# Attention and two feed-forward layers on one core: the second pair's operands in pieces, and two transpose banks lent as a third score buffer

## The chip, the cores and the metric

The kernel runs on one core of a Trainium2 chip. The metric is device microseconds (us) of one execution. Five engines work side by side, each through its own instruction queue in order: PE (TensorE, matmuls and transposes), DVE (VectorE), ACT (ScalarE), POOL (GpSimd) and SP (SyncE, which issues nearly all DMA transfers). PSUM, where PE writes, has eight banks of 128x512 float32; ACT and DVE read it.

## The reference

Attention over 4 batches of 8 heads (576 positions, head size 64), with rotary embedding of q and k, and then two feed-forward layers over the 2304 tokens.

```python
q_rot, k_rot = (rotate(q), rotate(k))            # x1*cos - x2*sin, x1*sin + x2*cos
scores = scale * np.matmul(q_rot, k_rot.transpose(0, 1, 3, 2))
attn = np.exp(scores - np.max(scores, axis=-1, keepdims=True))
attn = attn / (np.sum(attn, axis=-1, keepdims=True) + 1e-09)
x = np.matmul(attn, v)                           # then tokens x 512
...
h = x @ w_in;  g = s * np.maximum(h, 0)**2 + b;  x = g @ w_out        # 512 -> 2048 -> 512
g = x @ w_gate; silu = g / (1 + np.exp(-g)); x = (silu * (x @ w_val)) @ w_out2   # 512 -> 1536 -> 512
```

## The kernel before

Every float32 product is made from rounded halves: a value is split into a high part (fp32r) and the rest, and the products of the parts are added in PSUM. The 32 heads are worked as 16 pairs. For a pair p the steps are:

- **Preparation** (`prep`). q and k are loaded (tile x) and turned by the rotary tables (`rope`: four tensor operations, on DVE for the first pair, on POOL for the others) into the tile ry. PE transposes ry in three groups g = 0, 1, 2 of three blocks each (line 578, PSUM tile pst). For pair 0, ACT and DVE write the three operand tiles a (queries), t and kz (keys) straight from PSUM (lines 610 to 615). For all other pairs ACT writes the high part (qkhi, line 585) and DVE the rest (qklo, line 587), and SP then spreads them over the partitions with five DMA transfers a, a, t, t, kz (line 632). The operand tiles exist twice, for even and odd pairs.
- **Scores** (`pair`). A pair has nine chunks u = 0 to 8 of 128 queries. For each, PE multiplies a by t and kz (line 707: four matmuls 128x288, eight for u = 4) into a score buffer ps_s of two banks, DVE takes the row maximum (line 710, nm), ACT the exponential with its row sum (line 714, e). The buffer is free when ACT has read it.
- **Thirds** (`third`). For each three chunks PE transposes e back (lines 782 and 785: three groups of four 128x128 blocks and one of three 64x128) into a transpose bank ps_t; ACT writes the high part ph (line 790), DVE the rest (line 795: pl, or ph for the 64-row group); then the bank is free. PE multiplies by the values vh (lines 832 and 834, ps_av), ACT takes the result out (xr), SP stores it.

The eight banks are: three for transposes (`ps_t`, shared by the transposes of preparation and thirds, and later by feed-forward products), one for the values' product (`ps_v`), four for two score buffers (`ps_s`), which later become four accumulators of the feed-forward layers.

The order of instructions on every engine is not that of the code. A planner (`Schedule.run`) plays the program through with estimated durations, gives each engine the ready operation with the lowest priority number, hands out buffers by counting tokens, and emits the instructions in the order that comes out. A change in a buffer count or an operation's length therefore moves instructions all through the attention part. Short dummy matmuls (`warm`, line 463) fill PE at the start; eight each are tied behind chunk 1 and chunk 3 of the first pair. When the last pairs run out, first-layer products (hb, lines 938 to 940) fill PE; from there on PE has work without a break.

Of the kernel before, what the change touches and what calls it, by code (L numbers as in the profile page):

```python
# [187 lines left out]
def tile_attention_moe_moe(  # L188
# [54 lines left out]
        "xr": 2, "rbx": 1, "s": 2, "t": 3, "v": 1, "wx": 4, "gb": 2, "rb2": 3,  # L243
# [10 lines left out]
    ps_t = ctx.enter_context(tc.tile_pool(name="ps_t", bufs=3, space=PSUM))  # L254
# [5 lines left out]
    rp_p = early.enter_context(tc.tile_pool(name="rp", bufs=2, side="right"))  # L260
    att = ExitStack()
# [208 lines left out]
    first_rope, behind_rope, sts = [], [], {}  # L470

    qk_ops = list(sch.ops)

    def prep(p):
# [43 lines left out]
        for g in range(G):  # L518
# [8 lines left out]
            def r1(g=g, e=e, views=views, cs=cs):  # L527
                if g == 0:
                    take_ry()
                e.tensor_tensor(out=views(1)[1], in0=views(0)[0], in1=table(2, 1, cs.start, cs.stop), op=ALU.mult)  # L530
# [8 lines left out]
            if o is None and p:  # L539
                def y0():  # L540
                    take_ry()
                    if p == 1:
                        nc.gpsimd.tensor_copy(st["ryt"][:, 0, 0:1], first_rope[1]["ryt"][:, PC - 1, 2 * D - 1:2 * D])
                    nc.gpsimd.tensor_tensor(out=views2(0)[1], in0=views2(1)[0], in1=table(3, 1, 0, PC), op=ALU.mult)
# [35 lines left out]
            acq = (ps_tok, hi_tok if p else tok) if g == 0 else (ps_tok,)  # L580
# [26 lines left out]
            else:  # L607
# [15 lines left out]
                st.setdefault("a", []).append([o2, op("dve", t_dve(CG), sub(a[dn], a[up], up), prt + 3 * later, (o2,), (), (ps_tok,))])  # L623
                if p or g == 0:
                    ops += st["a"][-1]
        if p:
# [9 lines left out]
            ops = [  # L636
# [38 lines left out]
    def pair(p, st):  # L675
# [10 lines left out]
        for u in range(NU):  # L686
            pr = base + 10 * u
            s_tok = Token("s")
# [8 lines left out]
            def s_mm(u=u, terms=terms):  # L697
# [4 lines left out]
                ps = ps_s.tile([128, 1024], F32, tag="s", name="ps_s")  # L702
# [25 lines left out]

        sums[b]["exps"] += exps.values()
        if pp == H // 2 - 1:  # L730
# [7 lines left out]
            def r2():  # L738
                sums[b]["ps"] = ps_t.tile([128, 512], F32, tag="t", name="psr")
# [6 lines left out]
            tok, cr_tok = Token("t"), Token("cr")  # L746
# [14 lines left out]
        def third(y, pr):  # L761
# [11 lines left out]
            for i in range(4):  # L773
                t_tok = Token("t")
# [3 lines left out]
                def tr(i=i, part=part):  # L778
                    ps = st["pt", y, i] = ps_t.tile([128, 512], F32, tag="t", name="ps_t")
# [242 lines left out]

    def switch_0():
# [14 lines left out]
    def get_hb(tok, n):  # L1038
        p, tag = (ps_t, "t") if tok.pool == "t" else (ps_v, "v")
        return p.tile([128, 512], F32, tag=tag, name="hb")[:, 0:n]  # L1040
# [17 lines left out]
    def block_b():  # L1058
# [9 lines left out]
        fin = moe1(st, UB, range(F1), outs, x_toks, xp, prio, ("t", "v"), get_hb,  # L1068
# [166 lines left out]
    def block_s(i):  # L1235
# [19 lines left out]
        acc_tok = {(h, d): Token("t", "v") if (h, d) == (1, 0) else Token("acc") for h in range(2) for d in range(KD)}  # L1255
# [54 lines left out]
        def unit(u, pr):  # L1310
            t_g, t_5, t_m = (Token("rb2", "rc", "dec") for _ in range(3))
            banks, ps, prod = {x: Token("t", "v") for x in "xyz"}, {}, {}
# [174 lines left out]
    def block_2(i):  # L1487
# [27 lines left out]
        def bank(tok):  # L1515
            p, tag = (ps_t, "t") if tok.pool == "t" else (ps_v, "v")
            return p.tile([128, 512], F32, tag=tag, name="hb")[:, 0:QN]
# [49 lines left out]
        def unit(f, pr):  # L1567

            t_g, t_u, t_c, t_5 = (Token("rb2", "rc", "dec") for _ in range(4))
            banks, ps, prod = {x: Token("t", "v") for x in "xyz"}, {}, {}  # L1570
# [179 lines left out]
```

## Time and profile before

| | |
|---|---|
| median of 3 runs | 1081.68 us (1081.45 to 1081.71) |
| the profiled execution | 1081.71 us, its span 1079.9 us |
| PE busy | 1069.0 us, 99% of the span |
| DVE busy | 879.0 us, 81% |
| ACT busy | 732.0 us, 68% |
| POOL busy | 244.7 us, 23% |
| granted TensorE clock | 1.00 |

1.8 us lie around the span. The attention part is roughly the first 290 us; the rest belongs to the feed-forward layers. Busy time of PE counts each matmul to its modelled end, so that short gaps between matmuls of the attention part count as busy.

### The profile page before, as it was taken

To read this page: it belongs to the slowest core of one execution; us is meant where nothing else is said; L and a number is where in the kernel's file an instruction comes from. 1 tells how busy PE (TensorE), PEld (TensorE's weight loads), DVE (VectorE), ACT (ScalarE), POOL (GpSimd) and SP (SyncE) were. 2 spreads that over 40 slices of the span, in tenths; PEclk is the share of its full clock that TensorE was granted. 3 is DMA by queue.
4 is the path that set the end of the run, shared out by engine and by line. 5 is a ranking of instruction groups with operands and counts; after the bars stand their busy time and mean duration, and the time that the engine had idled before them with its cause. 6 is when DMAs were issued, how large, how long until landed. Compare 5 with 4: busy or idle time off the path is not lost.

```text
span 1079.9 us, 17714 instructions
## 1 busy us (share of the span) xinstructions
PE 1069.0 (99%) x6220; PEld 976.2 (90%) x6220; DVE 879.0 (81%) x1548; ACT 732.0 (68%) x1505; POOL 244.7 (23%) x239
## 2 busy tenths in 40 slices
PE   9999999999999999999999999999999999999998
PEld 8899998999888899999888888999989999899996
DVE  6899999999889999889999998876596675966751
ACT  6999999999978776556666556655565555655550
POOL 7997877887520000000000000000000000000000
PEclk9999999999999999999999999999999999999999
DMA  5766857656579655663566744311331222311102
GB/s 155 237 211 222 268 172 264 205 171 191 147 222 280 162 170 174 184 190 105 169 191 214 227 157 156 107 69 59 98 88 40 60 69 87 100 40 48 50 1 58
DMA packets 111593, 157.07 MB, mean 145 GB/s; under 512 B 34496, under 2 KB 67280, under 8 KB 111504
## 3 DMA queue, kind: packets, MB, share of 16 engines
q1 hardware_dynamic: 110688, 155.15, 46.2%
q8 instruction: 49, 0.80, 0.3%
q10 hardware_dynamic: 816, 0.79, 0.2%
q14 instruction: 40, 0.33, 0.1%
HBM read 99.98 MB, written 32.58 MB: 123 GB/s over the span
## 4 chain that ended last, share of the span: by engine, by line
PE 89%; ACT 4%; DVE 4%; issue 1%; DMA 1%; POOL 0%; SPq 0%; ACTq 0%; DVEq 0%
PE hb L938 14%; PE hb L940 14%; PE hb L939 14%; PE acc L939 6%; PE acc L940 6%; PE acc L938 5%; PE ps_s L707 5%; PE acc L1532 5%; PE acc L1533 5%; PE acc L1531 5%; PE ps_t L782 4%; PE ps_av L832 3%; PE ps_av L834 2%; ACT e L714 2%; ACT ph L790 1%; DVE pl L795 1%
## 5 line engine op out<-in xcount | busy, mean ns | idle before, releaser
L939 PE MATMUL hb<-w 128*128 128x384 f32 (+1 forms) x728 | 250.0, 343 | 0.0
L938 PE MATMUL hb<-w 128*128 128x384 f32 (+1 forms) x728 | 250.0, 343 | 0.0
L940 PE MATMUL hb<-w 128*128 128x384 f32 (+1 forms) x728 | 249.9, 343 | 0.0
L938 PEld LDWEIGHTS hb<-w 128*128 128x128 f32 x728 | 136.7, 188 | 8.4 <-ACT tmp L1592 0.2
L939 PEld LDWEIGHTS hb<-w 128*128 128x128 f32 x728 | 136.6, 188 | 7.5
L940 PEld LDWEIGHTS hb<-w 128*128 128x128 f32 x728 | 136.7, 188 | 4.4
L710 DVE TENSOR_REDUCE nm<-ps_s 128x1 f32<-128x576 f32 x144 | 108.0, 752 | 10.6 <-PE ps_s L707 9.3
L714 ACT ACTIVATE e<-ps_s,nm 128x576 f32<-128x576 f32 x144 | 107.4, 746 | 11.3 <-DVE nm L710 10.4
L790 ACT ACTIVATE ph<-ps_t 128x512 fp32r<-128x512 f32 (+1 forms) x183 | 101.2, 570 | 8.8 <-PE ps_t L782 7.3
L939 PE MATMUL acc<-gl,w 128*128 128x512 f32 (+1 forms) x288 | 106.0, 368 | 0.0
L940 PE MATMUL acc<-gh,w 128*128 128x512 f32 (+1 forms) x288 | 105.9, 368 | 0.0
L938 PE MATMUL acc<-gh,w 128*128 128x512 f32 (+1 forms) x288 | 105.9, 368 | 0.0
L707 PE MATMUL ps_s<-t,a 128*128 128x288 f32 x320 | 98.0, 323 | 2.0 <-ACT e L714 1.5
L832 PE MATMUL ps_av<-ph,vh 128*128 128x384 f32 (+1 forms) x320 | 96.5, 331 | 1.0 <-ACT xr L845 0.8
L795 DVE TENSOR_TENSOR pl<-ps_t,ph 128x512 fp32r<-128x512 f32 x135 | 90.0, 683 | 6.7 <-ACT ph L790 5.5
L1592 ACT ACTIVATE tmp<-hb 128x384 f32<-128x384 f32 x144 | 70.4, 489 | 34.5 <-PE hb L940 33.3
L707 PE MATMUL ps_s<-kz,a 128*128 128x288 f32 x320 | 88.9, 294 | 0.0
L782 PE MATMUL ps_t<-ident,e 128*128 128x128 f32 x576 | 85.5, 273 | 1.9 <-DVE pl L795 1.0
L782 PEld LDWEIGHTS ps_t<-ident,e 128*128 128x128 f32 x576 | 68.2, 141 | 8.8 <-DVE pl L795 1.9
L1230 DVE TENSOR_TENSOR w<-sums,w 128x512 fp32r<-128x512 f32 x104 | 68.4, 686 | 7.8 <-ACT w L1228 7.6
L834 PE MATMUL ps_av<-pl,vh 128*64 128x384 f32 (+1 forms) x256 | 72.3, 295 | 0.1
L1624 ACT ACTIVATE tmp<-tmp 128x384 f32<-128x384 f32 x72 | 37.7, 523 | 43.6 <-DVE tmp L1597 43.4
(145 smaller groups left out, 2478.1 us busy)
## 6 DMA issues: line engine op xcount, KB each, us to landing
raw<-gv SPq DMA_DIRECT2D x36, 512.0 KB, 3.7
raw<-in_moe_w_out_dram SPq DMA_DIRECT2D x28, 512.0 KB, 4.2
x_d<-xr SPq DMA_DIRECT2D x64, 144.0 KB, 2.5
raw<-in_moe_w_in_dram SPq DMA_DIRECT2D x16, 512.0 KB, 5.0
raw<-up SPq DMA_DIRECT2D x16, 512.0 KB, 4.3
raw<-in_moe_w_gate_dram SPq DMA_DIRECT2D x12, 512.0 KB, 4.8
raw<-in_moe_w_val_dram SPq DMA_DIRECT2D x12, 512.0 KB, 4.3
gv<-dec SPq DMA_DIRECT2D x24, 256.0 KB, 2.6
```

Of the source, the lines that this page charges most:

```text
L707: nc.tensor.matmul(ps[:, hf * 512:hf * 512 + HS], a[:, q0:q0 + 128], m[:, k0:k0 + HS], start=y == 0, stop=y == len(todo) - 1)
L710: nc.vector.tensor_reduce(out=st["nm"][:, u:u + 1], in_=st["s", u], axis=AX.XY, op=ALU.max, negate=True)
L714: nc.scalar.activation(out=st["e", u].rearrange("p (f n) -> p f n", f=2), in_=st["s", u], func=AF.Exp, bias=st["nm"][:, u:u + 1], accum_ou ...
L782: nc.tensor.transpose(ps[:, z * 128:z * 128 + 128], st["e", u][:, kc * 128:kc * 128 + 128], ident)
L790: nc.scalar.activation(out=st["ph", y][0:rows, 512 * i:512 * i + n], in_=st["pt", y, i][0:rows, 0:n], func=AF.Copy)
L795: nc.vector.tensor_tensor(out=dst, in0=st["pt", y, i][0:rows, 0:n], in1=st["ph", y][0:rows, c].bitcast(F32), op=ALU.subtract)
L832: nc.tensor.matmul(ps, vv, st["ph", y][:, c], start=kc == 0, stop=kc == 4, skip_group_check=True)
L834: nc.tensor.matmul(ps[0:64], vv[:, 0:64], st["pl", y][:, c], start=False, stop=False, skip_group_check=True)
L938: nc.tensor.matmul(o, lh, rh, start=first, stop=False, skip_group_check=more)
L939: nc.tensor.matmul(o, lh, rl, start=False, stop=False, skip_group_check=more)
L940: nc.tensor.matmul(o, ll, rh, start=False, stop=last, skip_group_check=more)
L1592: nc.scalar.activation(out=st[key, f], in_=ps[name], func=AF.Copy)
```

## The change

- **A third score buffer at first.** Of the three transpose banks one remains (`ps_t`). The two others are at the start one more score buffer, `ps_s0`, on the other side of PSUM. The transposed groups 1 and 2 of pair 0 go into its two halves; then chunk 2 of pair 0 uses it as its score buffer. When that chunk's exponential has read it, a switch (`switch_s0`) closes it and opens a pool t2 of two transpose banks, so that from there on there are three again; an operation takes one from t or t2, whichever is free (`BANKS`).
- **The second pair in pieces.** The rope of pair 1 runs on POOL as 3 x 4 operations, one set for each group, in place of four over all groups (a one-element copy that ordered it behind the first pair's rope remains), so that a group's transposes need its own four alone. Its spread transfers are 3 x 5, each for a group's 192 positions of both heads, and each needs its own group alone. Within a group the order is t, t, kz, a, a. The last group's two transfers of a are awaited by chunk 1 in place of chunk 0.
- **The order of pair 0's last subtractions on DVE** is set: t of group 2 ahead of a of group 1.
- Everything after takes the new names of the banks; the work of the feed-forward layers is the same.

```diff
-        "xr": 2, "rbx": 1, "s": 2, "t": 3, "v": 1, "wx": 4, "gb": 2, "rb2": 3,
+        "xr": 2, "rbx": 1, "s": 2, "s0": 1, "t": 1, "v": 1, "wx": 4, "gb": 2, "rb2": 3,
...
-    ps_t = ctx.enter_context(tc.tile_pool(name="ps_t", bufs=3, space=PSUM))
+    ps_t = ctx.enter_context(tc.tile_pool(name="ps_t", bufs=1, space=PSUM))
...
+    first_s = ExitStack()
+    ps_s0 = first_s.enter_context(tc.tile_pool(name="ps_s0", bufs=1, space=PSUM, side="right"))
...
+    def t_tile(tok, name):
+        return (ps_t if tok.pool == "t" else late[tok.pool]).tile([128, 512], F32, tag="t", name=name)
...
+            if p == 1:
+                def begin():
+                    take_ry()
+                    nc.gpsimd.tensor_copy(st["ryt"][:, 0, 0:1], first_rope[1]["ryt"][:, PC - 1, 2 * D - 1:2 * D])
+                if g == 0:
+                    o = op("pool", 0.1, begin, pr, (*lds[0], *rt_op, *first_rope[:1]), (ry_tok,))
+                for y, fn in enumerate((r0, r1, r2, r3)):
+                    o = op("pool", t_pool(fd if y > 1 else fd // 2), fn, pr + g, (o,), (), (x_tok,) if y == 3 else ())
+                st["rope"] = o
...
-            ps_tok = Token("t")
-            def tr(g=g):
-                st["ps", g] = ps = ps_t.tile([128, 512], F32, tag="t", name="pst")
+            if p == 0 and g:
+                ps_tok = s0_tok
+            else:
+                ps_tok = Token(*BANKS)
+            def tr(g=g, ps_tok=ps_tok):
+                if ps_tok is s0_tok:
+                    if g == 1:
+                        st["s0"] = ps_s0.tile([128, 1024], F32, tag="s", name="ps_s0")
+                    ps = st["s0"][:, 512 * (g - 1):512 * g]
+                else:
+                    ps = t_tile(ps_tok, "pst")
...
+                if g == 1:
+                    st["a1"] = st["a"][-1][1]
+                if g == G - 1:
+                    ops[-2].next.append(st["a1"])
+                    st["a1"].need += 1
...
-            ops = [
+            def piece(o, i, g):
+                return sch.dma(
+                    256 * 2 * S // G, lambda: nc.sync.dma_start(out=place(o, g).bitcast(F32), in_=place(i, g).bitcast(F32)), pr + 6 + g,
+                    (trs[g], *cleared), (tok,) if not ops else (), (hi_tok,), pace=1.1
+                )
+            for g in range(G if p == 1 else 0):
+                ops.append(piece(t[ev], lo_x[od], g))
+                ops.append(piece(t[od], hi_x[od], g))
+                ops.append(piece(kz[ev], hi_x[od], g))
+                ops.append(piece(a[ev], hi_x[ev], g))
+                ops.append(piece(a[od], lo_x[ev], g))
+            ops = ops or [
...
+        if p == 1:
+            st["a"], ops = ops[-2:], ops[:-2]
...
-            s_tok = Token("s")
+            s_tok = Token("s0" if p == 0 and u == 2 else "s")
...
-                ps = ps_s.tile([128, 1024], F32, tag="s", name="ps_s")
+                ps = (ps_s0 if p == 0 and u == 2 else ps_s).tile([128, 1024], F32, tag="s", name="ps_s")
...
+            if p == 1 and u == 1:
+                main = [*main, *st["a"]]
...
+        if p == 0:
+            op("sp", 0.0, switch_s0, -500, (exps[2],))
...
+    def switch_s0():
+        first_s.close()
+        pool("t2", 2, space=PSUM, side="right")
```

What the planner makes of it is shown at three places. The rows are instructions in queue order, with the line in the kernel's own file, the written tile, the tiles read and the shape.

The first place is DVE behind the first pair's operands: the maxima nm of pair 0 and the low parts qklo of pair 1. Before:

```order
L710 TENSOR_REDUCE nm<-ps_s 128x1 x5
L795 TENSOR_TENSOR pl<-ps_t,ph 128x512
L587 SCALAR_TENSOR_TENSOR qklo_184<-pst,ident,qkhi_182 128x2x192
L710 TENSOR_REDUCE nm<-ps_s 128x1
L587 SCALAR_TENSOR_TENSOR qklo_184<-pst,ident,qkhi_182 128x2x192 x2
L710 TENSOR_REDUCE nm<-ps_s 128x1
L795 TENSOR_TENSOR pl<-ps_t,ph 128x512 x2
L710 TENSOR_REDUCE nm<-ps_s 128x1
L795 TENSOR_TENSOR ph<-ps_t,ph 64x384
L710 TENSOR_REDUCE nm<-ps_s 128x1
```

Of the change:

```order
L752 TENSOR_REDUCE nm<-ps_s 128x1 x2
L611 SCALAR_TENSOR_TENSOR qklo_187<-pst,ident,qkhi_185 128x2x192
L752 TENSOR_REDUCE nm<-ps_s 128x1 x3
L611 SCALAR_TENSOR_TENSOR qklo_187<-pst,ident,qkhi_185 128x2x192
L752 TENSOR_REDUCE nm<-ps_s 128x1
L841 TENSOR_TENSOR pl<-ps_t,ph 128x512 x2
L752 TENSOR_REDUCE nm<-ps_s 128x1
L841 TENSOR_TENSOR pl<-ps_t,ph 128x512
L611 SCALAR_TENSOR_TENSOR qklo_187<-pst,ident,qkhi_185 128x2x192
L752 TENSOR_REDUCE nm<-ps_s 128x1
L841 TENSOR_TENSOR ph<-ps_t,ph 64x384
L752 TENSOR_REDUCE nm<-ps_s 128x1
```

Both pieces end with the maximum of pair 0's last chunk; in the change three pl, one ph and one pl follow, and then the maximum of pair 1's chunk 0. The first group of pair 1 has moved from behind chunk 4's maximum to between those of chunks 1 and 2, the second group ahead of the first third. On ACT the high part of the first group stands likewise between the exponentials of chunks 0 and 1, and on PE the group's transposes stand in the middle of the eight dummy matmuls behind chunk 1.

The second place is PE at the start of pair 2 (operands a_175, t_177, kz_179 before, a_178, t_180, kz_182 in the change). Before:

```order
L707 MATMUL ps_s<-t_177,a_175 128x288
L707 MATMUL ps_s<-kz_179,a_175 128x288
L707 MATMUL ps_s<-t_177,a_175 128x288
L707 MATMUL ps_s<-kz_179,a_175 128x288
L782 MATMUL ps_t<-ident,e 128x128 x4
L832 MATMUL ps_av<-ph,vh 128x384
L834 MATMUL ps_av<-pl,vh 64x384
L782 MATMUL ps_t<-ident,e 128x128 x4
```

Of the change:

```order
L828 MATMUL ps_t<-ident,e 128x128 x8
L749 MATMUL ps_s<-t_180,a_178 128x288
L749 MATMUL ps_s<-kz_182,a_178 128x288
L749 MATMUL ps_s<-t_180,a_178 128x288
L749 MATMUL ps_s<-kz_182,a_178 128x288
L749 MATMUL ps_s<-t_180,a_178 128x288
L749 MATMUL ps_s<-kz_182,a_178 128x288
L749 MATMUL ps_s<-t_180,a_178 128x288
L749 MATMUL ps_s<-kz_182,a_178 128x288
```

Before, chunk 0 of pair 2 stood ahead of five groups of pair 1's 128-row transposes and two 64-row groups, and these lay between the chunks of pair 2. Now all of pair 1's transposes but one 64-row group stand ahead of chunk 0, and chunks 0 and 1, then 2 and 3, follow each other. At the start of pair 3 both orders have issued the same work: 24 groups of 128-row transposes, 7 of 64 rows, 43 products with the values, 15 groups of preparation.

The third place is PE behind the last chunk of the last pair, where hb is the first layer's product. Before:

```order
L785 MATMUL ps_t<-ident,e 64x128 x3
L938 MATMUL hb<-x,w 128x512
L939 MATMUL hb<-x,w 128x512
L940 MATMUL hb<-x,w 128x512
L938 MATMUL hb<-x,w 128x512
L939 MATMUL hb<-x,w 128x512
L940 MATMUL hb<-x,w 128x512
L832 MATMUL ps_av<-ph,vh 128x192
L834 MATMUL ps_av<-pl,vh 64x192
L782 MATMUL ps_t<-ident,e 128x128 x4
```

Of the change:

```order
L831 MATMUL ps_t<-ident,e 64x128 x3
L828 MATMUL ps_t<-ident,e 128x128 x4
L878 MATMUL ps_av<-ph,vh 128x192
L880 MATMUL ps_av<-pl,vh 64x192
L878 MATMUL ps_av<-ph,vh 128x192
L880 MATMUL ps_av<-pl,vh 64x192
L828 MATMUL ps_t<-ident,e 128x128 x4
```

Twelve hb products that stood among the last third's transposes now stand behind them. In the feed-forward layers the order of PE's products changes in the first half and is the same from the middle to the end.

## Rows read from the trace of the kernel before

**Rows 1.** Stretches: length, busy time and instructions by engine, clock, DMA share, GB/s.

```profile
12.00:30.00 18.00, 16.39 (x130) 13.70 (x129) 14.07 (x23) 12.81 (x32) 17.84 (x13) 1.00 0.54 176
30.00:45.00 15.00, 14.46 (x117) 13.71 (x116) 13.72 (x23) 13.26 (x32) 14.18 (x12) 1.00 0.62 205
45.00:62.00 17.00, 16.69 (x133) 15.52 (x132) 15.38 (x25) 15.51 (x37) 17.00 (x11) 1.00 0.68 207
80.00:280.00 200.00, 197.43 (x1539) 183.99 (x1540) 187.45 (x295) 188.96 (x449) 158.16 (x163) 1.00 0.66 209
300.00:350.00 50.00, 50.00 (x223) 41.39 (x222) 44.65 (x74) 41.59 (x71) 5.92 (x7) 1.00 0.84 253
```

**Rows 2.** Waits, 13 to 64 us, DVE and ACT: total, times, longest.

```profile
DVE nm L710 <- PE ps_s L707: 3.2, 3, 1.6
ACT e L714 <- DVE nm L710: 5.5, 6, 2.1
```

**Rows 3.** Timeline, first pair: start, length, engine, line, operation, count, idle before.

```profile
13.53 1.42 DVE L710 TENSOR_REDUCE nm<-ps_s 128x1 f32<-128x576 f32 x2
14.32 0.74 ACT L714 ACTIVATE e<-ps_s,nm 128x576 f32<-128x576 f32 x1 [2.07 <-DVE nm L710]
15.20 0.40 PE L707 MATMUL ps_s<-t,a 128*128 128x288 f32 x1
16.03 1.49 DVE L710 TENSOR_REDUCE nm<-ps_s 128x1 f32<-128x576 f32 x2 [1.09 <-PE ps_s L707]
16.65 1.15 PE L463 MATMUL warm<-a 128*64 128x64 f32 x16
19.11 0.76 DVE L710 TENSOR_REDUCE nm<-ps_s 128x1 f32<-128x576 f32 x1 [1.59 <-PE ps_s L707]
20.04 0.58 ACT L585 ACTIVATE qkhi<-pst,ident 128x384 fp32r<-128x384 f32 x1
20.78 0.61 DVE L587 SCALAR_TENSOR_TENSOR qklo<-pst,ident,qkhi 128x384 fp32r<-128x384 f32 x1
```

**Rows 4.** Timeline of POOL: rope of pair 1 (first and last operation), clearing of kz.

```profile
10.31 1.41 POOL L544 TENSOR_TENSOR ry<-x,rt 128x576 f32<-128x576 f32 x1
15.88 2.69 POOL L552 TENSOR_TENSOR ry<-x,ry 128x1152 f32<-128x1152 f32 x1
34.42 1.14 POOL L629 MEMSET kz<- 128x1216 f32 x1
```

**Rows 5.** Pair 1's spread, first and last issue; a small load's KB and us to landing.

```profile
23.23 0.57 SPq L632 DMA_DIRECT2D a<-qkhi  x1
26.75 0.60 SPq L632 DMA_DIRECT2D kz<-qkhi  x1
vr<-in_v_dram SPq DMA_DIRECT2D x32, 80.0 KB, 2.5
```

**Rows 6.** Timeline: DVE at pair 0's end; PE at chunks 1.0, 2.0, 2.5.

```profile
28.44 1.29 DVE L795 TENSOR_TENSOR pl<-ps_t,ph 128x512 fp32r<-128x512 f32 x2 [0.68 <-ACT ph L790]
29.76 0.55 DVE L795 TENSOR_TENSOR ph<-ps_t,ph 64x384 fp32r<-64x384 f32 x1
...
31.04 0.38 PE L707 MATMUL ps_s<-t,a 128*128 128x288 f32 x1
...
45.06 0.38 PE L707 MATMUL ps_s<-t,a 128*128 128x288 f32 x1
...
55.32 0.29 PE L707 MATMUL ps_s<-t,a 128*128 128x288 f32 x1
```

**Rows 7.** Timeline, last pair: chunk 8, first hb, an ACT copy, the last transposes.

```profile
279.20 0.40 PE L707 MATMUL ps_s<-t,a 128*128 128x288 f32 x1
282.25 0.47 PE L938 MATMUL hb<-x,w 128*128 128x512 f32 x1 [0.26 <-DVE pl L795]
284.61 0.60 ACT L801 ACTIVATE raw<-ps_t 128x512 f32<-128x512 f32 x1 [1.31 <-PE ps_t L782]
288.33 0.49 PE L785 MATMUL ps_t<-ident,e 128*64 128x128 f32 x3
```

More of the change, by code (lines that the diff above doesn't have):

```diff
@@ L527, in r1 @@
             def r1(g=g, e=e, views=views, cs=cs):
-                if g == 0:
+                if g == 0 and p == 0:
                     take_ry()
@@ L579, in prep @@
             hi_x, lo_x = hi_t[z], lo_t[z]
-            acq = (ps_tok, hi_tok if p else tok) if g == 0 else (ps_tok,)
+            acq = (ps_tok, hi_tok if p else tok) if g == 0 else () if p == 0 and g == 2 else (ps_tok,)
             prt = pr + 3 + g
@@ L773, in third, with tr @@
             for i in range(4):
[L774 removed]
+                t_tok = Token(*BANKS)
                 part = blocks[4 * i:4 * i + 4]
                 n, rows = (512, 128) if part else (QT, 64)
[L778 to L779 removed]
+                def tr(i=i, part=part, t_tok=t_tok):
+                    ps = st["pt", y, i] = t_tile(t_tok, "ps_t")
                     if part:
@@ L1038, in get_hb @@
     def get_hb(tok, n):
-        p, tag = (ps_t, "t") if tok.pool == "t" else (ps_v, "v")
-        return p.tile([128, 512], F32, tag=tag, name="hb")[:, 0:n]
+        return (t_tile(tok, "hb") if tok.pool in BANKS else ps_v.tile([128, 512], F32, tag="v", name="hb"))[:, 0:n]
     ends = []
@@ L1067, in block_b @@
         toks = [Token("acc") for _ in range(KD)]
-        fin = moe1(st, UB, range(F1), outs, x_toks, xp, prio, ("t", "v"), get_hb,
+        fin = moe1(st, UB, range(F1), outs, x_toks, xp, prio, (*BANKS, "v"), get_hb,
                    toks, ("gb", "gc"), ("rb2", "rc"), lambda name: late[name], "act")
@@ L1254, in block_s @@
         hs, order = chains["gb"]
-        acc_tok = {(h, d): Token("t", "v") if (h, d) == (1, 0) else Token("acc") for h in range(2) for d in range(KD)}
+        acc_tok = {(h, d): Token(*BANKS, "v") if (h, d) == (1, 0) else Token("acc") for h in range(2) for d in range(KD)}
         y_need = {}
@@ L1311, in unit @@
             t_g, t_5, t_m = (Token("rb2", "rc", "dec") for _ in range(3))
-            banks, ps, prod = {x: Token("t", "v") for x in "xyz"}, {}, {}
+            banks, ps, prod = {x: Token(*BANKS, "v") for x in "xyz"}, {}, {}
             def product(z, name, when, deps=()):
@@ L1515, in bank @@
         def bank(tok):
-            p, tag = (ps_t, "t") if tok.pool == "t" else (ps_v, "v")
-            return p.tile([128, 512], F32, tag=tag, name="hb")[:, 0:QN]
+            return get_hb(tok, QN)
         a_toks = {(h, c): Token("acc") for h in range(2) for c in range(nt)}
@@ L1569, in unit @@
             t_g, t_u, t_c, t_5 = (Token("rb2", "rc", "dec") for _ in range(4))
-            banks, ps, prod = {x: Token("t", "v") for x in "xyz"}, {}, {}
+            banks, ps, prod = {x: Token(*BANKS, "v") for x in "xyz"}, {}, {}
             def product(z, name, when, deps=()):
```

11 lines of the change are left out of this document (6 added, 5 removed).

## The prediction

> **What bounds the kernel now.** I read the stretches first, then the waits of the start, then the timeline around each place that the change moves. From 300 us on PE is never idle [rows 1]: 223 matmuls of 0.224 us fill 50 us. The total is therefore the time at which the attention part hands over to that stretch, plus a fixed amount of PE work. The change has to win inside the attention part or not at all. There no engine is alone the bound: between 80 and 280 us DVE is busy 94% (187.45 of 200) and ACT 94% (188.96) [rows 1]. A chunk goes PE, DVE, ACT and back to PE, and what they lose is the latency of that round. The start is looser: in the three stretches from 12 to 62 us DVE is busy 43.17 of 50 us and ACT 41.58 [rows 1]. At 94% the same DVE work would take 45.9 us and the ACT work 44.2 us. So **about 4 us** is the most that a perfect start could give, and the losses have names: DVE waits 3.2 us for scores, ACT 5.5 us for maxima (2.1 of them ahead of the first exponential) [rows 2].
>
> One round of a score buffer follows from [rows 3]: scores at 15.20, their maximum at 16.03 (0.83 later); maximum at 13.53, its exponential at 14.32 (0.79); exponential at 14.32, the next scores in its buffer at 15.20 (0.88). Together 2.5 us, so two buffers give a chunk each 1.25 us when nothing else is between, while DVE needs 0.7 us for a maximum (two in 1.42) and ACT about as much.
>
> **The start: chunks 2 to 4 of pair 0.** Chunk 2 no longer waits for the exponential of chunk 0. It still stands behind the eight dummies, half of the 1.15 us that 16 records take [rows 3], and now behind group 0's transposes of pair 1, which need four POOL operations. Two POOL lengths, 1.41 us for 576 elements and 2.69 for 1152 [rows 4], give about 0.13 us plus 2.2 ns an element: 0.55 and 1.0 us for a third. Group 0 is ready at 10.3 + 3.1 = 13.4, the transposes run at about 13.8, chunk 2 at 14.5 in place of 15.20. But its maximum does not gain. On DVE it now stands behind qklo of that group, which waits for qkhi, which stands on ACT behind exponential 0: 14.32 + 0.73, then 0.58 [rows 3], so qklo runs from 15.7 to 16.25 and the maximum of chunk 2 starts at 16.25, 0.2 later than now (16.03). What is won comes behind it: chunk 4 is ready after the other eight dummies at 16.4, its maximum follows those of 2 and 3 at 17.75, **1.35 us earlier** than 19.11 [rows 3], and the two idle spaces of DVE (1.09 and 1.59) are filled by it and by preparation.
>
> **To the first scores of pair 1.** From there I add DVE's new order. Exponentials 2 and 3 on ACT end at 18.5, qkhi of group 1 at 19.0, so qklo runs at 19.1. Then one qklo (0.55), a maximum (0.7), two pl (1.29 for two [rows 6]), a maximum, a pl bring it to 22.45; the qklo of group 2 ends at about 23.3 with 0.3 of waiting. Two maxima, two ph of 0.55 [rows 6], four pl (5.1 us) and some 0.7 of waiting later comes pair 1's first maximum, 29.1, so its scores start at **28.3, 2.7 us earlier** than 31.04 [rows 6]. The transfers allow it. Now five whole ones are issued from 23.23 to 27.35 [rows 5]. In pieces, groups 0 and 1 are long gone, and behind qklo at 23.3 only t, t and kz of group 2 are needed. With an issue each 0.6 to 0.7 us the last of them leaves at about 25 us, and at the 2.5 us that a load of like size takes [rows 5] it lands at 27.5. The rope's eight more POOL operations cost 8 x 0.13 = 1 us there, and twice that if a short operation costs more than the line says; POOL's pair 2 is needed by PE at about 33 us and ready at about 32, so this is hidden by 1 us.
>
> Against fifteen transfers for five speaks the Trainium skill, DMA: Bandwidth & Descriptors, section Anatomy of one DMA: each transfer has a fixed cost of about 2.0 us, whatever its size. Ten more would be 20 us if they were paid one after the other. [Rows 5] show five issued within 4.1 us, so several are in flight and the fixed part is paid once at the end of the chain; taken by the page's fit the last piece lands 2.2 us after its issue, which leaves the sum as it is.
>
> **What pair 1 and 2 give back.** All three preparation groups of pair 2 now stand together behind pair 1's chunk 3. There qklo waits on DVE for an exponential and two qkhi on ACT, 0.73 + 2 x 0.5, against 0.55 of other work: about 1.1 us lost, **1.6 left**. Next, five 128-row groups and one 64-row group of pair 1's transposes have moved ahead of pair 2's chunk 0. They cost DVE 0.645 each, 3.5 us together, so chunk 0 of pair 2 starts at 45.06 - 1.6 + 3.5 = 47.0 [rows 6]. Its operands are there by then: the clearing of kz for them, 34.42 to 35.56 now [rows 4], stands behind one more rope operation of 2.7 us, so at about 38 us, and five issues and a landing end near 45. Then chunks 0 to 4 come with little between, and the round of the two buffers sets the pace: chunk 2 after 2.5 us, chunk 4 after 5.0, its eight matmuls and nine transposes another 2.3. Chunk 5 starts at 47.0 + 7.3 = 54.3, where it now starts at 55.32 [rows 6], with one preparation group more behind it (0.5 us on ACT, of which I count 0.2). **1.2 us are left.** At the start of pair 3 both orders have issued the same work, so that lead is carried on.
>
> **The later pairs and the end.** The order of later pairs changes too, in no direction that I can read; a tenth more or less of DVE's idle time between 80 and 280 us (12.55) is 1.25 us either way, and I take nothing. At the end twelve hb products, 12 x 0.224 = 2.7 us, no longer fill PE among the last transposes. Before, from chunk 8 to the last transposes it takes 9.1 us (279.20 to 288.33), and the hb products hold the transposes up there: ACT waits 1.31 us for one that stands behind six of them [rows 7]. Without them that stretch can be at most 2.7 shorter, which would make the two equal; if it gets no shorter, 2.7 us are lost. I take the equal case, because ACT and DVE are less busy there than PE's queue is long.
>
> The sum is -2.7 + 1.1 + 0.4 + 0.0 = -1.2 us on the profiled execution's 1081.71, and the median of the runs shown (1081.68) is the same number: **1080.5 us**. A measurement of this kernel can tell about 0.2%, 2.2 us, from no change, so this is mostly a forecast of "no difference that can be measured".
>
> **Rivals.**
> - *The lead is kept.* If chunks 0 to 4 of pair 2 run as dense as the rest, the 2.7 us of pair 1 are carried through: 1079.0 us. For it: ACT and DVE have idle time enough at the start (up to 4 us). Against it: the round of 2.5 us is measured, and nothing else stands between these chunks. Chance 0.24.
> - *The end loses its filler* (slower). PE stands idle 2.7 us among the last transposes, and the lead does not pay for it: 1081.7 - 1.2 + 2.7 = 1083.2 us. It decides from 1.2 us of idle PE there on. For it: the last third's transposes wait for an exponential, not for hb. Against it: the wait behind six hb products in [rows 7]. Chance 0.14.
> - *The start gives nothing.* If group 0's rope on POOL is later than 13.8 us, PE, in order, stands at its transposes and the whole first pair moves with it; 1 us more for each of its four operations cancels the lead: 1081.7 us. [Rows 4] give no operation that short. Chance 0.12.
>
> The forecast itself has 0.50, with 1079.3 to 1081.7 as its own range.
>
> **How the numbers follow.** Faster by over 0.2% (below 1079.5) takes most of the first rival (0.19) and an eighth of the forecast's own spread (0.06): 0.25. Slower by over 0.2% (above 1083.9) takes a third of the second rival and the tail of the others: 0.10. The rest, 0.65, is within 0.2%. The range reaches to the first rival with its spread, 1078.3, and just past the second, 1083.3.
>
> **What would show it.** In the changed profile: pair 0's chunk 2 maximum at or behind 16.0 us, chunk 4's near 17.7; pair 1's first scores near 28.3; pair 2's first scores later than now, near 47, and its chunk 5 near 54.3; POOL never waited for by PE; PE idle of 1 to 3 us behind the last pair's chunk 8, made up by an earlier last transpose. The prediction is wrong if pair 1's first scores do not come at least 1.5 us earlier, if pair 3 starts with a lead over 2.5 us or none, or if the later pairs' 200 us change by more than 1.3 us.

## The result, and the profile after

The changed kernel takes **1089.05 us** (1088.45 to 1090.97) against 1081.67 us for the kernel before on the same chip: a ratio of 1.0071, 95% interval 1.0061 to 1.0081. It is slower by 7.4 us, where 1080.5 was predicted and 1083.3 was the upper end. The profiled span is 1087.0 us (1079.9 before).

The stretches of the changed kernel, with the columns of [rows 1]:

```profile
12.00:30.00 18.00, 17.36 (x135) 14.54 (x135) 14.79 (x24) 13.63 (x34) 16.81 (x19) 1.00 0.50 150
30.00:45.00 15.00, 14.84 (x116) 13.91 (x116) 13.36 (x22) 13.27 (x32) 15.00 (x11) 1.00 0.58 171
45.00:62.00 17.00, 16.64 (x121) 14.07 (x121) 14.37 (x24) 14.24 (x35) 15.83 (x13) 1.00 0.87 272
80.00:280.00 200.00, 194.83 (x1513) 179.96 (x1511) 184.62 (x291) 185.79 (x442) 158.09 (x159) 1.00 0.65 209
```

Up to 30 us DVE and ACT do more than before (14.79 and 13.63 us against 14.07 and 12.81), so something is won there. From 45 to 62 us they do 1.0 and 1.3 less. And in the 200 us where the prediction expected no change, DVE stands idle for 15.38 us (12.55 before) and ACT for 14.21 (11.04).

The timeline of the first pair, in place of [rows 3]:

```profile
11.80 0.48 ACT L634 ACTIVATE a<-ps_s 64x384 fp32r<-64x384 f32 x1 [0.62 <-DVE t L639]
12.32 0.56 DVE L639 SCALAR_TENSOR_TENSOR t<-ps_s,t 64x384 fp32r<-64x384 f32 x1 [0.55 <-ACT a L634]
13.96 1.42 DVE L752 TENSOR_REDUCE nm<-ps_s 128x1 f32<-128x576 f32 x2
14.25 0.68 PE L470 MATMUL warm<-a 128*64 128x64 f32 x8
15.34 0.68 PE L470 MATMUL warm<-a 128*64 128x64 f32 x8
15.95 0.40 PE L749 MATMUL ps_s<-t,a 128*128 128x288 f32 x1
16.79 1.42 DVE L752 TENSOR_REDUCE nm<-ps_s 128x1 f32<-128x576 f32 x2
17.21 1.15 PE L470 MATMUL warm<-a 128*64 128x64 f32 x16
18.29 0.40 PE L749 MATMUL ps_s<-t,a 128*128 128x288 f32 x1
19.64 0.76 DVE L752 TENSOR_REDUCE nm<-ps_s 128x1 f32<-128x576 f32 x1 [1.43 <-PE ps_s L749]
```

Chunk 2's scores start at 15.95 (15.20 before), behind sixteen records of dummies and three transposes, not behind an exponential; chunk 4's at 18.29, directly behind sixteen more. Both maxima are later than before (16.79 against 16.03, 19.64 against 19.11). The first maximum is late too: ACT's a of group 2 waits 0.62 us for DVE's t of group 1, and DVE's t of group 2 waits 0.55 us for that a. The two groups lie in the two halves of one tile.

At the end of the attention part PE comes to its unbroken row of hb products. Before (one line), and in the changed kernel:

```profile
288.58 0.47 PE L938 MATMUL hb<-x,w 128*128 128x512 f32 x1
```

```profile
286.95 0.33 PE L878 MATMUL ps_av<-ph,vh 128*128 128x192 f32 x1 [0.28 <-POOL w L401]
289.83 0.36 PE L878 MATMUL ps_av<-ph,vh 128*128 128x192 f32 x1 [1.03 <-DVE ph L841]
291.43 0.47 PE L984 MATMUL hb<-x,w 128*128 128x512 f32 x1
```

Before, twelve hb products stood ahead of 288.58. They take 2.8 us (0.23 each), so at equal work of PE the changed kernel is 291.43 + 2.8 - 288.58 = 5.7 us late here, and 7.0 at the end of the span. Of the 1.3 us that are lost behind this place, 0.81 are one wait in the feed-forward layers; before has none there:

```profile
386.78 0.44 PE L984 MATMUL hb<-w 128*128 128x384 f32 x1 [0.81 <-ACT tmp L1383]
```

### The profile page after: what moved, and what is told of

Same layout as the page of the kernel before. It is cut to its first block, busy times and chain, and to the rows that moved or that the text cites. A ratio compares the mean times of both kernels' runs of the same rounds, so it can differ in the third digit from the quotient of the medians.

```text
span 1087.0 us, 17745 instructions
## 1 busy us (share of the span) xinstructions
PE 1072.9 (99%) x6220; PEld 975.6 (90%) x6220; DVE 881.4 (81%) x1548; ACT 733.2 (67%) x1505; POOL 244.4 (22%) x245
## 4 chain that ended last, share of the span: by engine, by line
PE 88%; DVE 7%; ACT 3%; issue 1%; DMA 1%; POOL 0%; SPq 0%; ACTq 0%; DVEq 0%
PE hb L984 14%; PE hb L986 14%; PE hb L985 14%; PE acc L985 5%; PE acc L984 5%; PE acc L986 5%; PE ps_s L749 5%; PE acc L1580 5%; PE acc L1581 5%; PE acc L1579 5%; PE ps_t L828 3%; PE ps_av L878 3%; DVE pl L841 2%; DVE nm L752 2%; PE ps_av L880 2%; ACT e L756 1%
## 5 line engine op out<-in xcount | busy, mean ns | idle before, releaser
L1640 ACT ACTIVATE tmp<-hb 128x384 f32<-128x384 f32 x144 | 70.4, 489 | 35.3 <-PE hb L986 33.6
L749 PEld LDWEIGHTS ps_s<-t,a 128*128 128x128 f32 x320 | 60.2, 188 | 9.1 <-ACT e L756 6.7
```

The costliest lines, as they stand in the source:

```text
L749: nc.tensor.matmul(ps[:, hf * 512:hf * 512 + HS], a[:, q0:q0 + 128], m[:, k0:k0 + HS], start=y == 0, stop=y == len(todo) - 1)
L1640: nc.scalar.activation(out=st[key, f], in_=ps[name], func=AF.Copy)
```

## The experiments

Two tables stand ahead, of the start of a chunk's maximum on DVE (us, from the timeline of each run's one profiled execution; "2.0" is pair 2, chunk 0). The very first maximum (0.0) lies between 13.9 and 14.65 us in eight runs whose order is the same up to there (changed, e1, e3, e4, e5, e8, e9, e10), so up to 0.7 us between two columns can be the execution alone. In the first table, all but the first column differ from before by:

| | before | changed | e1 | e9 | e3 | e4 |
|---|---|---|---|---|---|---|
| 1.0 | 31.9 | -1.4 | -1.3 | -1.3 | -0.9 | -0.9 |
| 2.0 | 46.0 | +4.3 | +4.4 | +4.4 | +4.8 | +4.8 |
| 3.0 | 64.0 | +1.1 | +1.2 | +1.2 | +1.7 | +1.6 |
| 10.0 | 184.0 | +0.5 | +1.2 | +1.7 | +1.0 | +0.9 |
| 12.0 | 216.5 | +1.5 | +1.1 | +1.7 | +4.7 | +1.9 |
| 13.0 | 232.9 | +4.5 | +1.2 | +1.7 | +4.4 | +5.2 |
| 15.8 | 280.8 | +3.3 | +1.3 | +1.8 | +4.5 | +5.0 |
| median less before's | | +7.4 | +1.4 | +2.5 | +3.8 | +4.5 |

| | before | changed | e6 | e7 | e12 | e13 | e14 | e16 |
|---|---|---|---|---|---|---|---|---|
| 0.0 | 13.5 | 14.0 | 14.0 | 13.6 | 14.2 | 13.5 | 13.3 | 13.6 |
| 0.2 | 16.0 | 16.8 | 16.2 | 16.6 | 16.9 | 16.0 | 16.0 | 16.3 |
| 0.4 | 19.1 | 19.6 | 19.1 | 20.3 | 18.5 | 19.1 | 17.6 | 19.3 |
| 1.0 | 31.9 | 30.5 | 33.7 | 29.2 | 29.6 | 31.9 | 28.8 | 28.5 |
| 1.8 | 44.1 | 44.1 | 46.5 | 42.7 | 43.1 | 44.1 | 42.3 | 41.9 |
| 2.0 | 46.0 | 50.3 | 48.5 | 48.9 | 49.4 | 46.0 | 48.6 | 48.1 |
| 2.5 | 57.1 | 58.0 | 58.5 | 56.4 | 57.0 | 57.1 | 56.2 | 55.7 |
| 3.0 | 64.0 | 65.1 | 65.8 | 64.5 | 64.2 | 64.0 | 63.4 | 63.7 |

**Whose order is used.** In all sixteen runs each engine takes its operations from a written list, made of what the planner gave for the one or the other kernel:

```diff
     def run(self):
+        turn = {e: deque(self.ops[i] for i in x) for e, x in orders().items()}
...
-                        item = heapq.heappop(ready[eng])
+                        item = next((x for x in ready[eng] if x[2] is turn[eng][0]), None)
```

**e1, the old order from pair 3.**

> The changed kernel keeps its own order up to the first scores of pair 3 (third score buffer, two transpose banks, fifteen small transfers all in it); from there on every engine issues what the kernel before issues, in its order. Theory A, the order that the planner chose behind the start costs the time: pair 3 starts 1.1 us later than before (65.1 against 64.0 us in the two traces), and nothing more is lost: 1081.7 + 1.1 = 1082.8 us. Theory B, the split into banks and small transfers costs by itself, wherever it is used (one bank and later two in a second pool instead of three in one): 1088 to 1089 us.

Measured: 1083.27 us, ratio 1.0014 (1.0005 to 1.0023). The 1.2 us of pair 3 stay 1.2 us for 217 us, to within 0.2: a lateness at pair 3 goes to the end one to one, and the banks and transfers cost nothing behind it. Theory B falls.

**e2, the new order from pair 3, on the kernel before.**

> The converse: the kernel before, with its three banks in one pool, its two score buffers and its whole transfers, in its own order up to the first scores of pair 3; from there on every engine issues in the order of the changed kernel. Theory A (order): what the changed kernel loses behind pair 3, 1089.05 - 1081.67 - 1.1 = 6.3 us, is lost here too: about 1088 us. Theory B (banks and transfers): 1081.7 to 1082.5 us.

Measured: 1090.70 us, 1.0076 (1.0059 to 1.0093), 8.8 us more than before in place of 6.3. 2.4 of it come at one place that the changed kernel does not have, and that the last section tells of; without it 6.4 us are left. The order alone, with nothing of the change in the kernel, loses what the changed kernel loses behind pair 3 (7.4 - 1.4 = 6.0 us).

**e3, e4 and e9, where behind pair 3 it is lost.**

> The changed kernel in its own order up to the first scores of pair 12, then in the order of the kernel before. Theory A: pair 12 starts 1.5 us late (218.0 against 216.5 us), the 3 us between pairs 12 and 13 and the 3 us at the end are not lost: 1083.2 us. Rival C, the 3 us between pairs 12 and 13 are not from the order but from DVE's decoding of weights running beside POOL's 2.59 us subtraction, which any order of these pairs meets: 1086 us.

> The changed kernel in its own order up to the last pair's last scores (chunk 8 of pair 15), then in the order of the kernel before, so that the hb products stand among the last transposes again. Theory A: the last scores come as late as in the changed kernel (3.3 us late by the maxima at 284.1 against 280.8), and what is lost behind them, 7.1 - 3.3 = 3.8 us, is not lost: 1085.2 us. Rival D, the end only passes on a lateness of the transposes, and the products give nothing: 1089 us.

> The changed kernel in its own order up to the first scores of pair 10, then in the order of the kernel before. The run that went back at pair 12 lost 2.7 us at that place, since the changed order had put off two decodes of weights and two more operations of DVE (about 2.6 us of its work) until behind pair 12's first maximum. At pair 10 it has put off next to nothing (one decode more, one correction less), so the maximum there, +0.5 us, is the true lateness. Theory A, what is lost behind pair 3 is lost between pairs 10 and 13, by the order: 1081.8 + 0.5 = 1082.3 us, up to 1083. Rival H, it is lost all along and only hidden in work put off: 1084 to 1085 us.

Measured: e3 1085.66 us (1.0035, 1.0022 to 1.0048), e4 1086.33 (1.0040, 1.0025 to 1.0055), e9 1084.02 (1.0020, 1.0011 to 1.0029). e4 gives back 2.7 us at the end, so rival D falls. e3 did not come out as theory A said: it loses nothing behind pair 12, but is 4.7 us late at pair 12's first maximum, since DVE had to do there what the changed order had put off. Rival C's time (1086) came out, not its place: in e3 the lateness does not grow between pairs 12 and 13. My reading of the trace, 3 us lost between pairs 12 and 13, was wrong: a maximum shows a lateness only where equal work lies ahead of it. In equal work the lateness is 1.2 us at pair 3, 1.7 at pair 10 (e9), 4.4 at pair 13 (e3) and 5.0 at the last maximum (e4; the changed kernel shows 3.3 there with work put off). The executions of e3 and e4 were already 1.6 to 1.7 us late at pair 3, so about 0.5 of their lateness was there before. So most of it, about 2.2 us, is lost between pairs 10 and 12. e9's median lies at rival H (1084 to 1085) and not at theory A (up to 1083): its maxima stay 1.7 to 1.8 us late, and in its profiled execution (1084.93, the slowest of ten) another 1.5 us are lost behind 290 us. The stretches between pairs 10 and 12, before (first two) and in the changed kernel:

```profile
184.00:200.40 16.40, 16.39 (x131) 15.65 (x131) 15.18 (x25) 15.04 (x37) 14.02 (x15) 1.00 0.68 222
200.40:216.50 16.10, 16.03 (x128) 15.15 (x126) 15.37 (x24) 15.67 (x38) 15.37 (x16) 1.00 0.73 234
```

```profile
184.40:201.90 17.50, 17.50 (x140) 16.49 (x139) 14.44 (x23) 16.17 (x41) 17.41 (x19) 1.00 0.67 217
201.90:218.00 16.10, 15.72 (x124) 14.62 (x123) 13.65 (x21) 14.77 (x37) 14.61 (x15) 1.00 0.71 229
```

DVE is idle 5.5 of 33.6 us, and was idle 1.95 of 32.5; PE is busy all the time in the first of them, with nine records more. DVE waits for PE:

```profile
195.81 0.82 PE L602 MATMUL pst<-ident,ry 128*128 128x128 f32 x6
196.82 0.49 PE L602 MATMUL pst<-ident,ry 128*128 128x128 f32 x3
197.15 0.60 PE L828 MATMUL ps_t<-ident,e 128*128 128x128 f32 x4
197.50 0.38 PE L749 MATMUL ps_s<-t,a 128*128 128x288 f32 x1
198.31 0.76 DVE L752 TENSOR_REDUCE nm<-ps_s 128x1 f32<-128x576 f32 x1 [1.31 <-PE ps_s L749]
```

Three groups of a later pair's preparation, nine transposes, stand on PE ahead of the scores that DVE waits 1.31 us for. With two more waits of DVE for scores (0.86 us ahead of 209.41 and 1.04 ahead of 215.93) these are 3.2 us; before, such waits were 0.55 and 0.33. That is most of DVE's additional idle time, but no run changed these places alone, so that they cause the loss is read from the trace and not shown.

**e5 and e8, two repairs that gave nothing.**

> The changed kernel in its own order only up to the first scores of pair 1, then in the order of the kernel before. Theory A (the order behind the start costs): the lead of 1.4 us that pair 1's first maximum has in the changed kernel (30.5 against 31.9 us) is no longer spent on pair 1's transposes ahead of pair 2, so it is kept: 1081.8 - 1.4 = 1080.4 us. Rival E, the lead is spent whatever the order, because pair 2's operands (POOL's rotation, transfers) are not ready earlier: 1081.8 us, or 1083 us where the fifteen transfers and the split rotation hold pair 2 up.

> The changed kernel in its own order, except for two instructions of DVE: two decodes of weights (1.23 and 1.49 us) that stand ahead of the correction ph and the first maximum of pair 13 go behind that maximum, one behind the next. Theory A: the 1.54 us that PE waits for ph and the 1.32 us that ACT waits for the maximum go, and most of the 3 us lost between pairs 12 and 13 (+1.9 at the last maximum of pair 12, +4.5 at the first of pair 13) come back: 1086 to 1087 us. Rival C, the decodes are as slow behind the maximum, beside POOL's other work, and hold up pair 13 from there: 1088 to 1089 us.

```diff
 DVE, from the last maximum of pair 12: mx, dec,
-dec, dec, ph, mx 13.0, pl, pl, mx 13.1
+ph, mx 13.0, dec, pl, pl, mx 13.1, dec
```

Measured: e5 1083.55 us (1.0014, 1.0004 to 1.0024). Pair 1 starts with no lead (31.9), pair 3 is 2.8 us late, and that stays: rival E. This execution is e5's slowest, and its first maximum is 0.7 us behind the changed kernel's; by the medians e5 is as late as e1 (1.0014 both). So the old order behind a start that was made for another one is no better than the new one. e8: 1089.78 us (1.0071, 1.0052 to 1.0089), nothing gained. Pair 13 starts 0.9 us earlier than in the changed kernel and ends 0.7 later; the lateness was work put off, not the place of the decodes.

**e6 and e7, the two parts of the change alone.**

> One part of the change alone: the third score buffer and the split of the transpose banks, with pair 1's rotation and transfers whole as before; planned anew up to the first scores of pair 3, then in the order of the kernel before. The question is which part loses the 1.2 us that the run with the old order from pair 3 kept to its end. Theory F, the buffer loses it (groups 1 and 2 of pair 0 share one tile and ACT and DVE take turns on it; the dummies stand ahead of chunks 2 and 4): 1083.0 us. Theory G, the pieces lose it (pair 1 starts early, then its transposes stand ahead of pair 2): 1081.8 us or less.

> The other part alone: pair 1's rotation in thirds and its fifteen small transfers, with two score buffers and three transpose banks in one pool as before; planned anew up to the first scores of pair 3, then in the order of the kernel before. Theory F (the buffer loses the 1.2 us): 1081.8 us or less. Theory G (the pieces lose it): 1083.0 us.

```diff
 e6, on the changed kernel
-            for g in range(G if p == 1 else 0):
+            for g in range(0):
 e7, on the kernel before
+            for g in range(G if p == 1 else 0):
+                ops.append(piece(t[ev], lo_x[od], g))
...
```

Measured: e6 1083.73 us (1.0017, 1.0007 to 1.0026), e7 1082.50 (1.0002, 0.9992 to 1.0012). Theory F holds. It is the pieces that bring pair 1 forward, by 2.7 us, to within 0.1 of what the prediction gave the whole change; the third buffer alone makes pair 1 1.8 us *later*. In e6 two more groups of the first third's transposes and the scores of chunks 5 and 6 go ahead of pair 1's preparation on PE, whose groups come at 21.54, 22.26 and 23.47 us (19.34 for two and 21.15 before), and the five transfers leave from 24.69 (23.23). In the changed kernel chunk 4 goes ahead of group 1's transposes on PE (19.44 us, 17.60 in e7). Its qklo and its transfers follow, on SP group 2 stands behind group 1, and its first issue (first block: changed; second: e7) is 2.1 us later.

```profile
26.49 0.60 SPq L667 DMA_DIRECT2D t<-qklo  x1
...
40.27 1.09 SPq L900 DMA_DIRECT2D x_d<-xr  x2
41.46 0.55 SPq L661 DMA_DIRECT2D a<-qkhi  x1
```

```profile
24.34 0.61 SPq L653 DMA_DIRECT2D t<-qklo  x1
...
38.12 0.49 SPq L647 DMA_DIRECT2D a<-qkhi  x1
...
41.65 1.82 SPq L884 DMA_DIRECT2D x_d<-xr  x2
```

The same blocks show pair 2's transfers: in the changed kernel they stand behind the store x_d, for which SP waits 4.0 us, and leave at 41.46 in place of 38.07.

**e10, e11 and e15, attempts to keep the lead ahead of pair 2.**

> The changed kernel in its own order up to the first scores of pair 2, then in the order of the kernel before, so that five of pair 1's transposes stand behind those scores again; and on SP the store x_d that stands ahead of pair 2's five transfers goes behind them (in the changed kernel they leave at 41.46 us behind that store, which waits 4.0 us for ACT's xr; before they leave at 38.07). Theory J, pair 2 starts late because its transfers stand behind that store and its scores behind pair 1's transposes: with both undone its first maximum comes at 45.5 to 47 us, the lead of 1.4 us is mostly kept, and the time is 1080.7 to 1081.7 us. Rival K, POOL's clearing of kz (38.17 us against 34.42) holds pair 2 by itself: first maximum at 48 us or later and 1083 us.

> Pair 1's rotation in thirds and its fifteen small transfers alone, with two score buffers and three transpose banks as before, in its own order up to the first scores of pair 2 (where pair 1 ends 1.4 us early: 42.7 against 44.1 us), then in the order of the kernel before. In the run with the pieces alone pair 2's transfers left at 38.12 us, as before. Theory J: pair 2's scores wait for the landing of kz alone, issued at 40.70 in place of 40.65 us, so its first maximum stays at 46 us, and what pair 1 is ahead by is lost there: 1081.7 us. Rival L, the shorter queue of work ahead of pair 2 lets its later chunks run denser: 1080.3 to 1081 us.

> The run before this one, and ahead of pair 2: on SP the store x_d goes behind pair 2's five transfers; on PE chunk 0 of pair 2 goes ahead of the last two groups of pair 1's transposes (four steps), its maximum on DVE ahead of two corrections and its exponential on ACT ahead of two steps. Theory J: pair 2's first maximum comes at 47.0 to 48.3 us (49.4 without), pair 3 starts 0.5 to 1.0 us earlier, and the time is 1080.2 to 1080.8 us, below the kernel before. Rival T, PE stands at chunk 0 until kz has landed, and what is won is lost behind it: 1081.3 us or more.

```diff
 SP
-put, sp, sp, sp, sp, sp, ld, ld
+sp, sp, sp, sp, sp, put, ld, ld
 PE (e15)
-tr, av, av, tr, tr, s_mm 2.0, s_mm 2.1
+tr, s_mm 2.0, av, av, tr, tr, s_mm 2.1
```

Measured: e10 1083.92 us (1.0021, 1.0012 to 1.0030), e11 1083.10 (1.0013, 1.0004 to 1.0022), e15 1082.30 (1.0006, 0.9997 to 1.0015). Each brings pair 2's first maximum forward (47.9, 47.2 and 47.1 us), and each has lost it one chunk later: 2.1 comes at 51.1, 50.9 and 49.9, where the runs that they were made from (changed, e7, e14) have 51.0, 49.5 and 49.2, with five groups of transposes ahead of pair 2 but two chunks close behind each other. Theory J's times at the end come out in none. e10 lies near rival K, but PE does not wait for kz there: it waits 1.00 us for a qklo of DVE ahead of pair 2's first scores (1.96 in e11). In e11 the granted clock fell as well, from 46.6 to 50.1 us (last section), so its chunk 2.1 is no test of the order alone. What holds pair 2 stays open.

**e12, e13, e14 and e16: what the third buffer needs.**

> The run with the old order from pair 3, without the sixteen dummy products ahead of chunks 2 and 4 of pair 0 (they compute nothing that is used). They take 0.68 + 0.68 us ahead of chunk 2's scores and 1.15 us ahead of chunk 4's in the changed kernel; the prediction had counted half of that. Theory M: without them chunk 2's first maximum comes at about 16.2 (16.8 with them) and chunk 4's near 18.0 (19.6), so the third buffer gives at last what the prediction put there; but pair 2 is held by other things, so the end moves little: 1082.5 to 1083.3 us. Rival N, PE's granted clock falls without the dummies, and the first pair gets slower: 1084 us or more.

> The kernel before, in its own order, without the sixteen dummy products in pair 0 (they compute nothing that is used). Theory P, the dummies were hidden there: chunk 2's scores wait for the exponential of chunk 0 anyway (15.20 us), and chunk 4's for that of chunk 2, which ends at 17.6 us, so their maximum comes 0 to 0.5 us earlier than 19.1, and the time is 1081.2 to 1081.5 us. Rival Q, they cost here what they cost in the changed kernel, 1.0 us or more: 1080.5 us.

> The run without dummies (1081.55 us), and groups 1 and 2 of pair 0 transposed into a tile of one bank each, in place of two halves of one tile; the third score buffer is opened in those banks for chunk 2. Theory R, the shared tile makes ACT and DVE take turns (waits of 0.62 and 0.55 us): without it the first maximum of pair 0 comes at 13.5 us (14.2), and 0.3 to 0.6 us of it reach the end: 1081.0 to 1081.3 us. Rival S, the next thing is late instead (the rotation of pair 1 on POOL, its transfers): 1081.5 us.

> The run with pair 1's pieces alone (two score buffers, three transpose banks; 1082.5 us, 0.5 us late at pair 3), without the sixteen dummies. Theory P (hidden while there are two score buffers): 1082.0 to 1082.5 us, so that the third buffer without dummies (1081.55) is worth 0.5 to 1 us. Rival Q (they cost the same everywhere): 1081.5 us, and the third buffer is worth nothing beside the pieces.

```diff
-    FILL = 8
+    FILL = 0
 e14 as well
-                        st["s0"] = ps_s0.tile([128, 1024], F32, tag="s", name="ps_s0")
-                    ps = st["s0"][:, 512 * (g - 1):512 * g]
+                    ps = ps_t0.tile([128, 512], F32, tag="t", name="pst0")
```

Measured: e12 1081.55 us (1.0003, 0.9994 to 1.0012), e13 1083.21 (1.0011, 1.0002 to 1.0020), e14 1082.09 (1.0004, 0.9995 to 1.0013), e16 1081.56 (0.9998, 0.9989 to 1.0007). Without the dummies the changed start (e12; e1 has them) is 1.1 us less late at pair 3, and all of it reaches the end: 1.4 us by the medians, each taken against before on its own chip, and 1.2 in the profiled executions. In the kernel before, the dummies cost nothing at the start: with them gone (e13) every maximum of pairs 0 to 3 is where it was, because PE then waits for the exponential instead:

```profile
15.21 0.40 PE L715 MATMUL ps_s<-t,a 128*128 128x288 f32 x1 [1.18 <-ACT e L722]
17.72 0.40 PE L715 MATMUL ps_s<-t,a 128*128 128x288 f32 x1 [0.98 <-ACT e L722]
```

e13's median stands 1.3 us above before's though its profiled execution took 1081.89 us, and the granted clock goes with it: the seven of its eleven executions from 1082.86 us up have a mean clock of 0.996 to 0.998, the four below that 0.999. None of the 104 executions of the kernel before beside these runs is under 0.999. e12's slowest, 1085.09 us, has 0.998. So the dummies seem to be of use in some executions of the kernel before; in which stretch the clock fell, no trace of these executions shows. With a tile for each group as well (e14) the start is the predicted one:

```profile
13.35 1.42 DVE L758 TENSOR_REDUCE nm<-ps_s 128x1 f32<-128x576 f32 x2
15.48 0.62 DVE L617 SCALAR_TENSOR_TENSOR qklo<-pst,ident,qkhi 128x384 fp32r<-128x384 f32 x1 [0.71 <-ACT qkhi L615]
16.02 1.41 DVE L758 TENSOR_REDUCE nm<-ps_s 128x1 f32<-128x576 f32 x2
17.60 0.76 DVE L758 TENSOR_REDUCE nm<-ps_s 128x1 f32<-128x576 f32 x1 [0.16 <-PE ps_s L755]
```

Chunk 2's maximum at 16.0, chunk 4's at 17.6 and pair 1's first at 28.8, where the prediction had 16.25, 17.75 and 29.1. Pair 3 is then 0.6 us early, and its profiled execution takes 1081.21 us; its median (1082.09) shows no gain. e16, the pieces without the third buffer, is as good, so the third buffer is worth nothing measurable beside them (rival Q). No version measured here is faster than the kernel before by more than the measurement can tell.

## Why the prediction was wrong

The medians split the 7.4 us: 1.4 up to pair 3 (e1), 3.1 from there to the last scores (e4 less e1), 2.7 at the end (changed less e4); the 0.2 that are left lie between the two chips. All three signs of being wrong that the prediction named came true: pair 1's first scores come 1.43 us earlier and not 1.5, pair 3 has no lead, and in the 200 us of the later pairs DVE is idle 2.8 us longer.

- **Start, "still stands behind the eight dummies, half of the 1.15 us"**: mis-sized. Each of the eight shows as two records (e12, without sixteen dummies, has 32 PE records fewer), so 1.15 us and not 0.6 stand ahead of chunk 2, and again ahead of chunk 4. [Rows 3] show the x16, and before it was hidden under the wait for the exponential (e13). I also left out that groups 1 and 2 in one tile make ACT and DVE wait for each other (0.62 and 0.55 us). With both undone, the other terms hold to 0.3 us (e14). For pair 1's first maximum that is in part luck: the terms from 19.1 us on add up to 23.0, not 22.45, and e14's shorter operations and waits make up for the slip.
- **Pair 1's first scores at 28.3**: came at 29.61. The mechanism of the pieces was right, and e7 shows it alone; behind the dummies, chunk 4 and then group 1's transposes came late. The fifteen transfers did no harm: PE waits for none of them in the changed kernel (0.43 us for one in e7). "kz", the slowest of them, takes 2.8 us to landing and "a" 2.0, several at once. By the Trainium skill, DMA: Bandwidth & Descriptors, section Anatomy of one DMA, a transfer issued by GpSimd has a fixed cost of about 2.0 us. These are issued by SP, and their rows are near that figure for one transfer and show that it is not paid one after the other.

```profile
kz<-qkhi SPq DMA_DIRECT2D x3, 96.0 KB, 2.8
a<-qkhi SPq DMA_DIRECT2D x3, 96.0 KB, 2.0
```

- **Pairs 1 and 2 give back 1.1 and 0.4**: mis-sized. They give back 1.4 and 1.1 in the changed kernel, and 1.4 and 1.2 also where the start is right (e14: 3.2 early at 1.0, 1.8 at 1.8, 0.8 at 2.5, 0.6 at 3.0; the prediction had 2.7, 1.6, 1.0 and 1.2). So a lead of 1.4 at pair 1 ended as a loss of 1.1 at pair 3. "Its operands are there by then" was wrong in the changed kernel: I followed POOL and kz, not the store ahead of the transfers on SP. It did not decide (e15); what made pair 2 so much dearer stays open.
- **"I take nothing" for the later pairs, 1.25 us either way**: the largest failure. The order behind pair 3 costs 3.1 us up to the last scores; with the end it is 5.8, and on the kernel before 6.4 (e2). I took the idle time of DVE and ACT in [rows 1] for a random quantity around which an order scatters by a tenth. As I read it now, it was the value of one good order, so that another could mostly lose; one other order was measured, which does not prove that.
- **The end, "made up, 0"**: the loss is 2.7 us, the second rival's price, but only a part of it lies where that rival put it. PE is idle for 1.31 us among the last transposes (0.28 and 1.03; 0.26 before), waiting for POOL and DVE. The last scores were 4.5 to 5.0 us late (e4, whose execution was already 0.5 behind the changed one at pair 3) and the unbroken row of hb 5.7, so 0.7 to 1.2 us are lost among the transposes; by this estimate most of the twelve products was indeed made up. The rest is lost behind them, against "plus a fixed amount of PE work": the wait of 0.81 us at 386.78, which stands in all three profiles with the changed order to the end (changed, e2, e8) and neither in before nor in e4, and 0.5 us in small pieces that no run follows.

The second rival had 0.14, with 1083.2 as its time. That its 2.7 us came out is in part luck, and it was combined with no loss in the later pairs.

## What to carry to other kernels

Where a planner orders the program, cost a local change twice: by its own mechanism, with the order of all else held fixed, and by what the new order does to every later stage; here the second (5.8 us) was four times the first (1.4). A filler that is free stands under a wait, so a change that takes the wait away has to take the filler too. And compare two orders only at points with equal work behind them: a first maximum that is early may have left work undone.

## What the runs showed of the hardware

An operation of DVE on 128x36 elements that takes 0.18 us took 2.65 us in e2, beside a POOL operation of 2.71 us: the first block is e2 (DVE, POOL), the second the changed kernel, where POOL waits for it by a small copy.

```profile
101.40 2.65 DVE L741 TENSOR_SCALAR l<-l 128x36 f32<-128x36 f32 x1
101.30 2.71 POOL L560 TENSOR_TENSOR ry<-x,ry 128x1152 f32<-128x1152 f32 x1
```

```profile
102.23 0.18 DVE L779 TENSOR_SCALAR l<-l 128x36 f32<-128x36 f32 x1
102.55 0.18 POOL L287 COPY seen<-l 128x1 uint32<-128x1 uint32 x1 [0.50 <-DVE l L779]
```

e2 has no such copy there, since the planner places it by its own times; that is e2's extra 2.4 us (its pair 6 starts 2.2 us late, pair 5 0.2 early). The Trainium skill, SBUF — State Buffer, section SBUF: two separate sides, says that DVE in some of its modes and POOL share a pair of ports that the first to start holds for the whole instruction. The rows agree: DVE ended at 104.05, POOL at 104.01.

PE's granted clock stayed at 1.00, the level of 2.4 GHz, in the profiled execution without the dummies (e14, with the columns of [rows 1]), although PE was idle for 0.54 us from 12 to 16 us and 0.29 in the next four:

```profile
12.00:16.00 4.00, 3.46 (x19) 2.45 (x19) 3.23 (x6) 1.95 (x6) 3.77 (x6) 1.00 0.67 194
16.00:20.00 4.00, 3.71 (x27) 3.24 (x27) 3.27 (x6) 3.31 (x11) 3.84 (x5) 1.00 0.34 99
```

In e11, which has the dummies, it fell to 0.50, the level of 1.2 GHz, from 46.6 to 50.1 us. Ahead of that PE was busy for 2.64 of 4.60 us, with one wait of 1.96 us (the columns of [rows 1]):

```profile
42.00:46.60 4.60, 2.64 (x21) 2.29 (x20) 2.49 (x5) 3.10 (x8) 4.52 (x6) 1.00 0.84 262
46.70:50.00 3.30, 3.30 (x16) 2.78 (x14) 3.04 (x5) 2.67 (x6) 3.30 (x2) 0.50 0.84 279
```

A group of four transposes started there took 1.06 us (47.71), against 0.60 at 50.65. e11's mean clock over this execution is 0.998, and so it is in five of its eleven executions (1083.10 to 1083.69 us; the other six 1082.39 to 1083.11, at 0.999 or 1.00).
